# A chunked linear-attention kernel with a fused MLP: N of the chunk after next earlier in the order, its inverse stored by GpSimd, turned w ahead of the decay sums

## The chip, the cores and the metric

The kernel runs on one core of one Trainium2 chip. The metric is the device time of one execution in microseconds (us). A core has five engines that run side by side, each with its own instruction queue: TensorE (PE; its weight loads are shown apart as PEld), VectorE (DVE), ScalarE (ACT), GpSimd (POOL) and SyncE (SP), which here issues nearly all DMAs. Each queue is worked off in the order of the program.

## What is computed

Two blocks in a row. The first is a recurrence over 768 steps for 4 batches and 8 heads with a 40x40 state. The second is an MLP over 3072 tokens with an exact GELU.

```python
for t in range(S):                       # batch 4, n_heads 8, seq 768, head_dim 40
    kt, vt, rt = (k[:, :, t], v[:, :, t], r[:, :, t])
    wt, at, bt = (w[:, :, t], a[:, :, t], b[:, :, t])
    y[:, :, t] = np.einsum('bhd,bhde->bhe', rt, state)
    Sa = np.einsum('bhde,bhe->bhd', state, at)
    state_decay = state * wt[:, :, None, :] - np.einsum('bhd,bhe->bhde', Sa, bt)
    state = state_decay + np.einsum('bhd,bhe->bhde', vt, kt)
...
h = x @ w_in                             # x: y turned to (3072, 320); w_in: (320, 2048)
g = 0.5 * h * (1.0 + erf(h * inv_sqrt2))
return g @ w_out                         # w_out: (2048, 320)
```

## The kernel before

The sequence is cut into 12 chunks of 64 steps. Within a chunk the recurrence becomes products of small matrices; between chunks only the state goes on. The dependence of the steps of one chunk on each other is a strictly triangular matrix N per batch and head, and the kernel needs the inverse of the unit triangular matrix that belongs to it. 64 such matrices of 64x64 per chunk are inverted in two steps: the 32x32 blocks on the diagonal on GpSimd, and the corner between them on TensorE.

The order of every engine's queue is the order in which the program is written: the kernel turns the planner off for all five engines (`manual_schedule`) and interleaves by hand. The loop over `c` (line 1122) works on three chunks at once: chunk `c` itself, `n = c + 1` whose inverse is finished, and `n2 = c + 2` whose inputs are loaded and whose N is made. The MLP of a finished chunk is a generator (`mlp`, line 894) of eight pieces; each `fill()` issues the next piece. In the steady state the first four pieces are the first layer (`ph`, line 902, 40 matmuls each), the last four the second layer. For chunks from 3 on the second layer is done with seven half-size products in place of eight (`seven`, line 845): m1 and m2, then m5 and m6, then m3 and m7, then m4, at line 855. A pair of them takes about 4.5 us of TensorE. For chunks 0 to 2 it is the plain product (line 919), whose PSUM buffer is held over four pieces.

The steps that the change touches:

- `sums(c)`, line 407: from the logarithms of w, two sets of products on TensorE, the running sums (`cum`, four matmuls) and the same turned (`wT_ps`, 64 matmuls); then on ScalarE the exponentials `rw` (line 420), `wp` (422) and, for chunks from 4 on, `en` (427).
- `scale_b` (460, DVE), `scale_k` (467, GpSimd): b and k times `rw`. `scale_a` (477, DVE): turned a times `wp`. `turn_b` (489): turned b times `en`, two DVE instructions (176 and 495).
- `make_N(c)`, line 572: 64 matmuls, then DVE masks them into N (line 550), then SP issues four DMAs that write the diagonal blocks to DRAM (line 587).
- `start_inverse(c, nc.gpsimd)`, line 623: GpSimd clears W, SP reads the blocks back in another layout (Nb, line 636), and GpSimd does 31 columns of two operations each (lines 644 and 646).
- `store_inverse(c)`, line 652: two DMAs write W to DRAM (line 658), each of 64 partitions, with runs of 128 bytes on the DRAM side. `fetch_inverse(c)`, line 661: six DMAs read it back (lines 668 and 672) into Tt and T2.
- `turn_corner(c)`, line 679: one DVE transpose of Tt into L (line 681). `corner(c)`, line 683: 64 small matmuls J of N and L, the first work of TensorE in the next turn of the loop.
- `make_A`, `make_av`, `make_RV` for chunk n: 64 matmuls each; A and RV are masked by DVE (line 550), av is copied by ScalarE (line 618). A(n) and the turned b of n2 share one SBUF buffer.

PSUM is handed out as four buffers of two banks each (`duo`, line 90), and every product above takes one.

In the order before, SP meets, per turn: the loads of w, a, r, turned b, v and turned k of n2; eleven DMAs inside SBUF for x (lines 803 and 806); the store of the inverse of n; the loads of v, b and k of n2 (lines 200 and 153); the fetch of the inverse of n; one store of results; the stores of N of n2; the reads of Nb; another store of results.

Of the kernel before, what the change touches and what calls it, by code (L numbers as in the profile page):

```python
# [19 lines left out]
def kernel(  # L20
# [69 lines left out]
    def duo(name):  # L90
        return psum.tile([P, 2, 512], FP32, tag="duo", name=name)
# [7 lines left out]
    def mm(o, lhsT, rhs, first=True):  # L99
        nc.tensor.matmul(o, lhsT, rhs, start=first, stop=True, skip_group_check=True)  # L100
# [295 lines left out]
    def run(steps):  # L396
        for _ in steps:
            pass
# [7 lines left out]

    def sums(c):
        logw = raws.pop((c, "w"))
        cum = duo("cum")[:, :, :DM]
        for g in range(G):  # L410
            mm(cum[:, g], cum_m, logw[:, g * DM:(g + 1) * DM])

        pt = duo("wT_ps").rearrange("p e (n t) -> p e n t", t=C)
        for n in range(G * NP):
            for x in range(2):
                for e in range(2):
                    at = (2 * n + x) * D
                    mm(pt[half(x), e, n], logw[half(e), at:at + HP], cum_m[half(e), half(e)])
        rw = (avs_ring if c in (1, 2) else part_ring)()[:, :, :DM]
        nc.scalar.activation(rw, cum, ACT.Exp, scale=-1.0)  # L420
        wp = wp_ring()
        nc.scalar.activation(wp[:, :, 1:].rearrange("p (n e) t -> p e n t", e=2), pt, ACT.Exp)
        decays[c] = rw.rearrange("p g (h d) -> p g h d", h=H), wp
        turned_in.setdefault(c, {})["wp"] = wp
        if c >= NB:
            en = turned_in.setdefault(c, {})["en"] = by_batch(side("en", "kT", 1))
            nc.scalar.activation(en.rearrange("p (e n) t -> p e n t", e=2), pt, ACT.Exp, scale=-1.0)

    def flip(src, name):

# [414 lines left out]
    def seven(c, s1, s2):  # L845
        t1, t2, t4 = sums_of_w
        t3 = quarter(0, 1)
        os = [work.tile([P, 2, DM // 2], FP32, tag="os", name="os", bufs=2) for g in range(G)]
        c11, c12, c21, c22 = os[0][:, 0], os[0][:, 1], os[1][:, 0], os[1][:, 1]

        def products_of(*factors):
            po = duo("po")
            for n, (l_, r_) in enumerate(factors):
                for f in range(NF // 2):
                    nc.tensor.matmul(po[:, n, :DM // 2], l_[:, f], r_[:, f], start=f == 0, stop=f == NF // 2 - 1)  # L855
            return po[:, 0, :DM // 2], po[:, 1, :DM // 2]

        def add(to, one_, other):
            nc.vector.tensor_tensor(to, one_, other, ALU.add)  # L859

        def store(g):
            for e in range(2):
                row = (G * e + g) * S + c * C
                nc.sync.dma_start(out=out[row:row + C], in_=os[g][half(e)].rearrange("p z d -> p (z d)"))

        m1, m2 = products_of((block(0, 0), quarter(0, 0)), (block(0, 1), quarter(1, 0)))
        if s2 is None:
            s2 = SM_ring().rearrange("p e g n c -> p (e g n c)")[:, :NF * P // 2].rearrange("p (f t) -> p f t", t=P)
            nc.vector.tensor_tensor(s2, s1, block(0, 0), ALU.subtract)
        nc.vector.tensor_tensor(block(1, 0), block(0, 0), block(1, 0), ALU.subtract)  # L870
        nc.scalar.copy(c12, m1)
        nc.scalar.copy(c11, m2)
        add(c11, c11, c12)
        yield
        nc.vector.tensor_tensor(block(0, 1), block(0, 1), s2, ALU.subtract)  # L875
        m5, m6 = products_of((s1, t1), (s2, t2))
        nc.scalar.copy(c22, m5)  # L877
        add(c12, c12, m6)
        yield
        m3, m7 = products_of((block(0, 1), quarter(1, 1)), (block(1, 0), t3))  # L880
        add(c21, c12, m7)
        add(c12, c12, c22)
        add(c12, c12, m3)
        add(c22, c22, c21)
        store(0)
        yield
        m4, _ = products_of((block(1, 1), t4))
        add(c21, c21, m4)
        store(1)
        yield  # L890
# [3 lines left out]
    def mlp(c):  # L894
        xt = xts.pop(c)
        for q in range(NF // 4):
            ph = duo("ph").rearrange("p x (s t) -> p x s t", s=2)
            for s in range(2):
                p = 2 * q + s
                for kt in range(NK):  # L900
                    for x in range(2):
                        nc.tensor.matmul(ph[:, x, s], w_in_sb[half(x), kt, p * P:(p + 1) * P], xt[half(x), kt],  # L902
                                         start=kt == 0, stop=kt == NK - 1)
            nc.scalar.activation(gt[:, 4 * q:4 * q + 4].rearrange("p (x s) t -> p x s t", x=2), ph, ACT.Gelu)  # L904
            if c >= NS and q == NF // 4 - 1:
                s1, s2 = half_tile("conv", 2), None
                nc.vector.tensor_tensor(s1, block(1, 0), block(1, 1), ALU.add)  # L907
                if c >= NCH - 2:
                    s2 = half_tile("conv", 2)
                    nc.vector.tensor_tensor(s2, s1, block(0, 0), ALU.subtract)  # L910
            yield
        if c >= NS:
            yield from seven(c, s1, s2)
            return
        po = duo("po")[:, :, :DM]
        for part in range(2):
            for g in range(G):
                for f in range(NF // 2 * part, NF // 2 * (part + 1)):
                    nc.tensor.matmul(po[:, g], gt[:, f, g * P:(g + 1) * P], w_out_sb[:, f],  # L919
                                     start=f == 0, stop=f == NF - 1)  # L920
                if part:
                    os = work.tile([P, DM], FP32, tag="os", name="os", bufs=2)
                    nc.vector.tensor_copy(os, po[:, g])  # L923
                    for e in range(2):
                        row = (G * e + g) * S + c * C
                        nc.sync.dma_start(out=out[row:row + C], in_=os[half(e)])
                yield

# [193 lines left out]
    for c in range(2, NCH):  # L1122
        n, n2 = c + 1, c + 2
        more, more2 = n < NCH, n2 < NCH
        corner(c)
        make_X(c)
        if c == NS + 1:
            weight_sums(3)
        if c == 2:

            seconds(1, (14, 14), last=True)
            fill()
            turn_b(n)
            make_N(n)
            run(start_inverse(n, nc.gpsimd))
            load_r(n)
            load_v(n)
        else:
            fill()
        if more2:  # L1140
            load_next(n2)
        joined(c)
        if c == 2:
            pieces.reverse()
            seconds(2, last=True)
        fill()
        make_sa(c)
        make_saT(c)
        if c == 2:
            turn_r(n)  # L1150
            scale_k(n, nc.vector)
            fill()
            pieces.reverse()
            fill(2)
            turn_k(n)
        if more2:
            load_r(n2)
        if more2:
            turn_a(n2)
            fetch_pairs(n2, "b_turned", b, nc.sync, False, paired["a"])  # L1160
        fill()
        make_y2(c)
        make_M(c)
        if more:
            turn_v(n)
        if more2:
            load_v(n2)
            turn_r(n2)
            fetch_pairs(n2, "k_turned", k, nc.sync, False, paired["r"])
        fill()  # L1170
        if more2:
            logs(n2)
        make_QY(c)
        outputs(c)
        pieces.append(mlp(c))
        fill()
        if c == NS:
            weight_sums(0)
            weight_sums(1)
        if more:  # L1180
            make_A(n)
            store_inverse(n)
        if more2:
            load_VR(n2)
            load_kb(n2)
            sums(n2)
        if more:
            turn_state()
        if more2:
            scale_a(n2)  # L1190
        fill()
        if more:
            fetch_inverse(n)
            make_av(n)
        if c == NS:
            weight_sums(2)
        if more2:
            turn_b(n2)
        if more:
            make_RV(n)  # L1200
        if more2:
            scale(n2)
        fill()
        if more:
            turn_corner(n)
        if more2:
            make_N(n2)
            run(start_inverse(n2, nc.gpsimd))
        if more2:
            turn_k(n2)  # L1210
        fill()
# [31 lines left out]
```

## Time and profile before

| | us |
|---|---|
| median of 3 runs | 751.65 |
| lowest, highest | 749.77, 757.06 |
| the profiled execution, its own time | 747.88 |
| its span, first to last instruction | 746.2 |
| PE busy | 677.1 (91%) |
| PEld, DVE busy | 588.7, 385.7 |
| POOL, ACT busy | 333.0, 214.3 |
| mean granted TensorE clock | 0.933 |

The profile is of one execution. A line of a timeline gives start, duration, engine, line of the kernel, operation, the tile written and the tiles read, and how many instructions were merged; in brackets the idle time of the engine before it and what ended it. "SPq" is the queue in which SP issues DMAs: its durations are those of the issue, not of the transfer. "PEclk" is the TensorE clock that was granted, 1.00 or 9 and more tenths being full.

### The profile page before, as it was taken

To read this page: it belongs to the slowest core of one execution; us is meant where nothing else is said; L and a number is where in the kernel's file an instruction comes from. 1 tells how busy PE (TensorE), PEld (TensorE's weight loads), DVE (VectorE), ACT (ScalarE), POOL (GpSimd) and SP (SyncE) were. 2 spreads that over 40 slices of the span, in tenths; PEclk is the share of its full clock that TensorE was granted. 3 is DMA by queue.
4 is the path that set the end of the run, shared out by engine and by line. 5 is a ranking of instruction groups with operands and counts; after the bars stand their busy time and mean duration, and the time that the engine had idled before them with its cause. 6 is when DMAs were issued, how large, how long until landed. Compare 5 with 4: busy or idle time off the path is not lost.

```text
span 746.2 us, 31351 instructions
## 1 busy us (share of the span) xinstructions
PE 677.1 (91%) x14096; PEld 588.7 (79%) x14096; DVE 385.7 (52%) x541; ACT 214.3 (29%) x279; POOL 333.0 (45%) x776
## 2 busy tenths in 40 slices
PE   7356889669999999999997999989999979999997
PEld 5355678557777877898896898887998978998987
DVE  2777389873335365474544464643563653531403
ACT  5124463523141241332231332232232312112020
POOL 3385168700831852842842833834833833810000
PEclk9655799679999999999998999998999998999999
DMA  9797659453756657556646565656556553030000
GB/s 120 131 178 139 122 120 237 80 116 81 130 108 125 110 106 131 99 107 129 117 79 116 106 106 116 120 86 132 100 99 129 102 88 64 16 57 4 20 18 19
DMA packets 302159, 75.76 MB, mean 102 GB/s; under 512 B 290408, under 2 KB 295304, under 8 KB 302024
## 3 DMA queue, kind: packets, MB, share of 16 engines
q1 hardware_dynamic: 301824, 73.58, 52.5%
q8 instruction: 111, 1.82, 1.0%
q14 instruction: 24, 0.20, 0.1%
q10 hardware_dynamic: 200, 0.16, 0.1%
HBM read 59.54 MB, written 10.22 MB: 93 GB/s over the span
## 4 chain that ended last, share of the span: by engine, by line
PE 49%; POOL 14%; SPq 13%; DMA 7%; DVE 7%; issue 6%; ACT 2%; ACTq 1%; DVEq 0%; POOLq 0%
PE ph L902 20%; PE po L919 7%; PE po L855 6%; POOL W L646 6%; POOL tmp L644 5%; SPq L153 4%; PE QY L100 3%; DMA Nb<-N 2%; DMA Tt<-inv 2%; SPq L668 2%; PE X L100 2%; PE J L100 2%; DMA N<-N 2%; SPq L806 1%; SPq L200 1%
## 5 line engine op out<-in xcount | busy, mean ns | idle before, releaser
L902 PE MATMUL ph<-xt,w_in_sb 64*128 64x256 f32 x1920 | 227.1, 389 | 0.7 <-ACT gt L904 0.4
L902 PEld LDWEIGHTS ph<-xt,w_in_sb 64*128 64x128 f32 x1920 | 186.9, 191 | 26.3 <-issue 1.8
L644 POOL TENSOR_TENSOR tmp<-W,Nb 128x126 f32<-128x126 f32 (+22 forms) x310 | 127.3, 411 | 137.6 <-DMA Nb<-N 114.0
L646 POOL TENSOR_TENSOR W<-W,tmp 128x126 f32<-128x126 f32 (+22 forms) x310 | 131.5, 424 | 24.3
L904 ACT ACTIVATE gt<-ph 128x1024 f32<-128x1024 f32 x48 | 49.1, 1023 | 149.2 <-PE ph L902 124.3
L855 PE MATMUL po<-w_out_sb,gt 128*128 128x160 f32 x576 | 82.9, 302 | 0.1
L855 PEld LDWEIGHTS po<-w_out_sb,gt 128*128 128x128 f32 x576 | 78.7, 190 | 2.2 <-DVE gt L875 0.4
L919 PE MATMUL po<-w_out_sb,gt 128*128 128x320 f32 x192 | 57.4, 454 | 0.6 <-DVE os L923 0.6
L471 POOL TENSOR_TENSOR k_rows<-k_rows,part 128x640 f32<-128x640 f32 x8 | 12.4, 1549 | 98.4 <-DMA Tt<-inv 86.8
L919 PEld LDWEIGHTS po<-w_out_sb,gt 128*128 128x128 f32 x192 | 37.0, 198 | 16.6 <-issue 2.3
L550 DVE TENSOR_TENSOR SM<-M_ps,upper 128x1024 f32<-128x1024 f32 x12 | 14.7, 1223 | 49.6 <-PE M_ps L100 49.6
L711 DVE COPY Tt<-J 32x512 f32<-32x512 f32 x12 | 8.3, 689 | 60.4 <-ACT Tt L711 60.3
L695 ACT COPY Js<-J 128x256 f32<-128x256 f32 x12 | 4.5, 371 | 100.5 <-PE J L100 100.5
L907 DVE TENSOR_TENSOR half<-gt 128x1024 f32<-128x1024 f32 x9 | 11.6, 1285 | 38.6 <-ACT gt L904 38.6
L100 PE MATMUL J<-L,N 32*32 32x32 f32 x768 | 10.2, 205 | 22.4 <-DVE L L681 22.4
L100 PEld LDWEIGHTS J<-L,N 32*32 32x32 f32 x768 | 8.9, 116 | 25.0 <-issue 25.0
L904 ACT ACT_TABLE_LOAD x10 | 12.8, 1283 | 47.7 <-PE ph L902 47.7
L303 ACT ACTIVATE conv<-conv,rebias 128x320 uint32<-128x320 uint32 (+1 forms) x26 | 16.0, 624 | 35.5 <-DVE conv L302 35.3
L859 DVE TENSOR_TENSOR os<-os,po 128x160 f32<-128x160 f32 x36 | 11.5, 319 | 28.2 <-ACT os L877 14.2
L855 PE MATMUL po<-extra,half 128*128 128x160 f32 x176 | 25.4, 299 | 0.0
L739 DVE COPY SM<-sap 128x640 f32<-128x640 f32 x12 | 9.9, 824 | 28.2 <-PE sap L100 28.1
L855 PEld LDWEIGHTS po<-extra,half 128*128 128x128 f32 x176 | 24.2, 190 | 0.0
(196 smaller groups left out, 1129.2 us busy)
## 6 DMA issues: line engine op xcount, KB each, us to landing
Nb<-N SPq DMA_DIRECT2D x22, 256.0 KB
VR<-in_v_dram SPq DMA_DIRECT2D x24, 160.0 KB
out_dram<-os SPq DMA_DIRECT2D x48, 80.0 KB
w_tile<-in_w_dram SPq DMA_DIRECT2D x22, 160.0 KB
b_rows<-in_b_dram SPq DMA_DIRECT2D x22, 160.0 KB
k_rows<-in_k_dram SPq DMA_DIRECT2D x22, 160.0 KB
w_out_sb<-in_moe_w_out_dram SPq DMA_DIRECT2D x11, 320.0 KB
N<-N SPq DMA_DIRECT2D x48, 64.0 KB
```

The lines of the kernel that those rows point to most:

```text
L100: nc.tensor.matmul(o, lhsT, rhs, start=first, stop=True, skip_group_check=True)
L153: eng.dma_start(out=t[half(e)].rearrange("p g h d -> p (g h) d")[:, :, :D], in_=rows_of(src, c, e))
L303: nc.scalar.activation(power, power, ACT.Relu, bias=rebias, scale=8.0)
L471: eng.tensor_tensor(to, raws.pop((c, "k")), rwv, ALU.mult)
L550: nc.vector.tensor_tensor(to, pt, upper.unsqueeze(1).to_broadcast([P, 2 * G * NP, C]), ALU.mult)
L644: eng.tensor_tensor(t, W[:, :rows, j:j + 1].to_broadcast([P, rows, rest]), Nb[:, j:j + 1, j + 1:].to_broadcast([P, rows, rest]), ALU.mult)
L646: eng.tensor_tensor(W[:, :rows, j + 1:], W[:, :rows, j + 1:], t, ALU.add)
L668: engs[j % len(engs)].dma_start(out=flat(Tt)[at:at + BL, :, z * BL:(z + 1) * BL], in_=inv[j, z].rearrange("n s t -> s n t"))
L855: nc.tensor.matmul(po[:, n, :DM // 2], l_[:, f], r_[:, f], start=f == 0, stop=f == NF // 2 - 1)
L902: nc.tensor.matmul(ph[:, x, s], w_in_sb[half(x), kt, p * P:(p + 1) * P], xt[half(x), kt], start=kt == 0, stop=kt == NK - 1)
L904: nc.scalar.activation(gt[:, 4 * q:4 * q + 4].rearrange("p (x s) t -> p x s t", x=2), ph, ACT.Gelu)
L919: nc.tensor.matmul(po[:, g], gt[:, f, g * P:(g + 1) * P], w_out_sb[:, f], start=f == 0, stop=f == NF - 1)
```

## The change

In `sums`, the turned products and their exponentials come first, and the sums and `rw` last. In the loop, `make_av(n)` with the fetch moves ahead of the second pair of half products, `turn_b(n2)` too, and `make_N(n2)` with the start of its inverse moves ahead of the third pair; `scale(n2)` now follows N. The store of the inverse is issued by GpSimd directly behind the inverse, where SP issued it a turn later. In `seven`, m5 and m6 are issued before one subtraction; in the plain second layer both halves are copied out and stored after the last product.

```diff
     def sums(c):
         logw = raws.pop((c, "w"))
-        cum = duo("cum")[:, :, :DM]
-        for g in range(G):
-            mm(cum[:, g], cum_m, logw[:, g * DM:(g + 1) * DM])
-
         pt = duo("wT_ps").rearrange("p e (n t) -> p e n t", t=C)
...
-        rw = (avs_ring if c in (1, 2) else part_ring)()[:, :, :DM]
-        nc.scalar.activation(rw, cum, ACT.Exp, scale=-1.0)
+        cum = duo("cum")[:, :, :DM]
+        for g in range(G):
+            mm(cum[:, g], cum_m, logw[:, g * DM:(g + 1) * DM])
         wp = wp_ring()
         nc.scalar.activation(wp[:, :, 1:].rearrange("p (n e) t -> p e n t", e=2), pt, ACT.Exp)
-        decays[c] = rw.rearrange("p g (h d) -> p g h d", h=H), wp
         turned_in.setdefault(c, {})["wp"] = wp
         if c >= NB:
             en = turned_in.setdefault(c, {})["en"] = by_batch(side("en", "kT", 1))
             nc.scalar.activation(en.rearrange("p (e n) t -> p e n t", e=2), pt, ACT.Exp, scale=-1.0)
+        rw = (avs_ring if c in (1, 2) else part_ring)()[:, :, :DM]
+        nc.scalar.activation(rw, cum, ACT.Exp, scale=-1.0)
+        decays[c] = rw.rearrange("p g (h d) -> p g h d", h=H), wp
...
+        m5, m6 = products_of((s1, t1), (s2, t2))
         nc.vector.tensor_tensor(block(0, 1), block(0, 1), s2, ALU.subtract)
-        m5, m6 = products_of((s1, t1), (s2, t2))
         nc.scalar.copy(c22, m5)
...
-                if part:
+                for last in range(G if part and g else 0):
                     os = work.tile([P, DM], FP32, tag="os", name="os", bufs=2)
-                    nc.vector.tensor_copy(os, po[:, g])
+                    nc.vector.tensor_copy(os, po[:, last])
                     for e in range(2):
-                        row = (G * e + g) * S + c * C
+                        row = (G * e + last) * S + c * C
                         nc.sync.dma_start(out=out[row:row + C], in_=os[half(e)])
...
             run(start_inverse(n, nc.gpsimd))
+            store_inverse(n, (nc.gpsimd,))
             load_r(n)
...
         if more:
             make_A(n)
-            store_inverse(n)
         if more2:
             load_VR(n2)
             load_kb(n2)
             sums(n2)
         if more:
             turn_state()
+            fetch_inverse(n)
+            make_av(n)
         if more2:
             scale_a(n2)
+            turn_b(n2)
         fill()
-        if more:
-            fetch_inverse(n)
-            make_av(n)
         if c == NS:
             weight_sums(2)
-        if more2:
-            turn_b(n2)
         if more:
             make_RV(n)
         if more2:
+            make_N(n2)
             scale(n2)
-        fill()
+            run(start_inverse(n2, nc.gpsimd))
+            store_inverse(n2, (nc.gpsimd,))
         if more:
             turn_corner(n)
-        if more2:
-            make_N(n2)
-            run(start_inverse(n2, nc.gpsimd))
+        fill()
         if more2:
             turn_k(n2)
         fill()
```

## The prediction

> **What bounds the kernel now.** I read the page first. Its busy line and its 40 slices show TensorE nearly full after the first fifth of the span:
>
> ```profile
> PE 677.1 (91%) x14096; PEld 588.7 (79%) x14096; DVE 385.7 (52%) x541; ACT 214.3 (29%) x279; POOL 333.0 (45%) x776
> PE   7356889669999999999997999989999979999997
> ```
>
> The reader is to see three slices below 9 late in the PE row: TensorE sets the pace and stops now and then. So I asked for the waits of PE from 280 us to the end (columns: total us, times, longest). There is one line only:
>
> ```profile
> PE J L100 <- DVE L L681: 11.9, 3, 4.1
> ```
>
> J (`corner`) waits for L, the turned corner of the inverse (`turn_corner`). Next I cut the span at the starts of J, one stretch per chunk (columns: us, busy time by engine, then PEclk):
>
> ```profile
> 289.20:340.20 51.00, 51.00 (x1181) 46.15 (x1180) 27.17 (x33) 15.51 (x20) 27.29 (x64) 1.00 0.62 114
> 340.20:395.70 55.50, 51.52 (x1181) 46.30 (x1181) 29.28 (x35) 15.50 (x20) 29.76 (x69) 1.00 0.59 109
> 395.70:450.40 54.70, 54.61 (x1180) 48.40 (x1180) 29.41 (x35) 15.50 (x20) 27.67 (x66) 0.94 0.58 107
> 450.40:505.30 54.90, 51.14 (x1181) 46.19 (x1181) 28.55 (x35) 15.51 (x20) 28.17 (x63) 1.00 0.57 109
> 615.40:665.70 50.30, 50.27 (x1048) 45.70 (x1048) 21.41 (x28) 9.77 (x14) 27.23 (x66) 0.94 0.22 43
> ```
>
> The first row is a chunk without loss: 51.0 us. The second waits 4 us at its end at full clock; the third does not wait, but its clock is 0.94 and it costs the same 3.7 us. They alternate. The timeline of PE shows why:
>
> ```profile
> 395.70 0.74 PE L100 MATMUL J<-L,N 32*32 32x32 f32 x64 [3.98 <-DVE L L681]
> 396.37 1.82 PE L100 MATMUL X<-st,aT 40*64 40x40 f32 x64
> 398.12 7.61 PE L902 MATMUL ph<-xt,w_in_sb 64*128 64x256 f32 x40
> 406.35 4.59 PE L902 MATMUL ph<-xt,w_in_sb 64*128 64x256 f32 x40
> ```
>
> Straight after the wait the same 40 matmuls take 7.61 us instead of 4.59, and X takes 1.82 instead of 1.14. This slow stretch gives the inverse the time that it lacks, so the next J finds L ready; the clock is then full, and the one after waits again.
>
> **Why L is late.** The loop of the inverse, from the timelines of POOL, SP and DVE (start, duration):
>
> ```profile
> 350.62 0.24 POOL L644 TENSOR_TENSOR tmp<-W,Nb 128x31 f32<-128x31 f32 x1 [9.86 <-DMA Nb<-N]
> 382.22 0.23 POOL L646 TENSOR_TENSOR W<-W,tmp 128x16 f32<-128x16 f32 x1
> 382.47 1.30 SPq L658 DMA_DIRECT2D inv<-W  x2
> 383.87 2.60 SPq L200 DMA_DIRECT2D VR<-in_v_dram  x2
> 389.88 2.45 SPq L668 DMA_DIRECT2D Tt<-inv  x4
> 394.86 0.70 DVE L681 STREAM_TRANSPOSE L<-Tt 128x512 f32<-128x512 f32 x1
> ```
>
> GpSimd ends the inverse at 382.45, 31.8 us after it began. SP stands at the store until then and issues it; behind it in SP's order are the loads of v, b and k, so the fetch of the inverse starts at 389.88, 7.4 us after the end. From there to the end of L are 5.7 us. The other half: N is masked at 340.57, its stores begin at 340.60, and GpSimd starts on it at 350.62, 10.0 us later. N's stores stand in SP's order behind the fetch and behind one output store (338.61 to 339.8).
>
> **The change, part by part.** Times count from a J, with 51.0 us to the next; the base is the chunk from 289.2.
>
> 1. *N ahead of m3 and m7.* N's products ended at 337.9; ahead of them now goes no third pair (4.5 us), so they end near 333.2. What N needs is ready: scale_a and turn_b move up too, 1.23 + 1.25 + 1.22 us of DVE behind the exponentials, done near 329.0. On DVE the mask no longer follows turn_corner, scale_b and four L859 additions, so N is masked near 334.3 instead of 340.57. SP now sets the start: it reaches the fetch 1.4 us earlier (the store left its queue), at 333.0, issues its six DMAs until 337.1, then N's four stores, 3.5 us earlier than before. GpSimd starts at 347.1, which is 6.9 after the next J instead of 10.4.
>
> 2. *The store on GpSimd.* Two DMAs, each of 64 partitions in 1024 runs of 128 bytes. Queued behind them on GpSimd are scale_k and the cleared W of the next chunk; these wait for k and then the new N for over 10 us anyhow (POOL idle 10.78 us before k_rows), so gain nothing and lose nothing below that. SP gets 1.3 us and no longer stands at the store with v, b and k behind it (five waits on W, 15.2 us in all). No POOL DMA is in this trace. Nearest row: the store of an earlier chunk, issued by an SP that stood ready; W ended at 146.20 and its landing released POOL's memset at 150.15, so **4.0 us** from end to landing. The page "DMA: Bandwidth & Descriptors" of the Trainium skill (Latency and other measured facts) gives about 1 us to the first byte for a GpSimd DMA and 0.6 on the SP path; by it an estimate of 4.4. But the page "SBUF — State Buffer" (A bandwidth-pool intuition that's wrong) speaks against this edit: GpSimd cannot write descriptors while DVE runs a two-port operation, 3.1 us in place of 0.62. For two DMAs that is 5 us more, 9.4. The DVE rows near the end of the inverse are masks, additions and tensor_tensor, with no copy, so I lean to the lower. Below 4.0 I see no reason (the same bytes land by the same 16 engines). What 2048 runs cost in software neither row nor page prices; I let the upper end be 15 us, SP's 1.3 us taken tenfold. I take **5**.
>
> 3. *The loop that follows.* GpSimd 31.8, store 5, fetch issue 4.1, N to GpSimd 10.0: 50.9 us against 51.0. In place of the 7.4 us between W and fetch stand 5. From 6.9: end at 38.7, landed at 43.7; SP comes to the fetch at 43.8; L 5.7 later at 49.5, less 0.9 of additions that no longer precede it (by the chain Tt landed at 393.93, L began at 394.86). J at 51.0 need not wait. **Gain**: the five stretches 340.2 to 615.4 come to 275.2 us, at 51.0 each 255.0: 20.2. The last row carries the slow clock alone, 3.2. Sum **23.4 us**; the earlier stall before the loop (5.8 us at 159.6) is untouched.
>
> 4. *av ahead of m5 and m6.* The 4.5 us pair covered A's mask. Now turned w (1.1), sums (1.3) and the state's turn (1.0) cover it: A's products end at 321.7, av could start at 325.1, the mask ended at 324.15. Covered, with 0.9 to spare; without that cover up to 1 us per chunk.
>
> 5. *Turned w first.* Inside the loop wp and en come about a microsecond earlier, rw later; scale_b has long waited for b instead. m5's PSUM buffer may wait for en: 0.15 us times seven. In chunks 2 and 3 one buffer of four is held by the long product, and av waits about 1.1 us twice (my estimate from exponentials of 1.28 + 1.03 + 1.03). In the first chunk rw moves from 9.12 to about 10.1; scale_b, then nT by TensorE, lose 0.3 us. Sum **2.7 us**, between 0 and 8.
>
> 6. m5 and m6 issued before the subtraction, and both copies of the long product after its second half: the same instructions on each queue; nothing waits between them. Zero; if the copies were late, 0.5 us in two chunks.
>
> Together: 23.4 - 2.7 = 20.7 us. The profiled execution took 747.88 us (span 746.2); it becomes about 727.2. The median of the three runs is 751.65, 3.8 above it; taken along, **731 us**.
>
> **Rivals.**
> *A, GpSimd's store is too dear (slower).* The loop is 45.9 + s, s from W's end to landing. From s = 5.1 a chunk waits, and each microsecond of s costs one per chunk. The chunks now average 55.0, so at s = 9.1 the change only breaks even. At s = 13 a chunk takes 58.9, six of them +23 us: 775. For: 2048 short runs by software, no row; DVE is 52% busy. Against: the gaps between GpSimd's operations are 0.07 us, and nothing queued behind needs it at once.
> *B, in part.* s of 6 to 8: chunks of 52 to 54 us, waits of 1 to 3 us. At 53 that is 2 x 6 = 12 us, plus the clock of the last chunk: about 739. A wait of 1.03 us in chunk 2 (before tn) left matmuls at normal length, so short waits should not cost clock.
> *C, SP stays the bound (same).* SP's rows in this chunk sum to about 44 of 51 us, and from the v loads (22.6 after J) to the end of the fetch there is no gap. If the earlier N meets longer issues (r loads vary from 3.94 to 6.55 us), small waits return, and with them the clock: 748 to 752.
>
> **How the numbers follow.** Full gain, 726 to 735: 0.42. B, 735 to 744: 0.20. C and the middle of A: 0.12. A, slower by over 7.5 us: 0.26. From 726 to 764 takes in all but 0.05 below and about 0.15 of A above; the likeliest alone is 726 to 735. One per cent (7.5 us) is about what a measurement of this kernel can tell, its runs being 749.77 to 757.06. Faster 0.62, same 0.12, slower 0.26.
>
> **What would show it.** Right: no J <- L line for PE after 280 us, stretches of 51 us at clock 1.00, N masked some 6 us before J, GpSimd starting 6 to 7 us after it, and landing within 5 us of W's end. Wrong: fetches on SP waiting for inv by POOL's queue for over 4 us (A), av or m5 as new waits of PE (parts 4 and 5), or L late with the landing long done (C).

## The result, and the profile after

| | before | after |
|---|---|---|
| median of 4 runs each | 752.15 | **727.96** |
| lowest, highest | 749.77, 757.06 | 725.91, 732.97 |
| profiled execution, its span | 747.88, 746.2 | 726.3, 724.5 |
| PE, POOL busy | 677.1, 333.0 | 663.1, 352.8 |
| mean granted TensorE clock | 0.933 | 0.946 |

The ratio is 0.968, with a 95% interval of 0.9608 to 0.9753: faster by 2.5 to 3.9%. 731 was forecast, with 726 to 735 as the likeliest stretch. Some executions are slower for reasons outside the kernel: the ratios here and below leave them out, the medians do not, and the profile of e12 below, taken in one of them, is not compared.

First the page of the changed kernel: its busy line, its PE slices, its clock, and the two DMA queues of data.

```profile
PE 663.1 (92%) x14096; PEld 582.5 (80%) x14096; DVE 383.5 (53%) x541; ACT 213.8 (30%) x279; POOL 352.8 (49%) x794
PE   6455889569999999999999999999999999999997
PEclk9655799779999999999999999999999999999999
q1 hardware_dynamic: 283104, 71.22, 52.0%
q0 software_dynamic: 864, 2.36, 1.8%
```

The three weak slices of PE are gone, and behind the prologue no digit of the clock is below 9. GpSimd's stores are the new queue q0. PE has the same 14096 matmuls and is busy 14 us less: that part of the gain is mostly clock. The rest is mostly waits. The waits of PE from 230 us on (total us, times, longest):

```profile
PE J L100 <- DVE L L680: 3.4, 4, 1.0
PE av L100 <- DVE A L549: 1.0, 1, 1.0
```

J still waits for L, but four times for at most 1.0 us where it waited three times for up to 4.1. The stretches from J to J (us, busy time by engine, PEclk, DMA share, GB/s), with two rows and then one left out by "...":

```profile
285.70:336.40 50.70, 50.70 (x1181) 46.18 (x1180) 28.41 (x35) 15.42 (x20) 30.02 (x68) 1.00 0.65 117
...
437.90:489.50 51.60, 50.77 (x1181) 46.17 (x1181) 28.61 (x34) 15.40 (x20) 31.73 (x68) 1.00 0.61 115
...
541.40:594.80 53.40, 52.49 (x1185) 47.45 (x1189) 28.42 (x35) 15.41 (x20) 32.07 (x68) 0.97 0.60 112
594.80:644.20 49.40, 47.80 (x1049) 43.51 (x1050) 20.74 (x28) 9.77 (x14) 27.78 (x64) 1.00 0.22 44
```

The clock is 1.00 in all but one, and a chunk without loss takes 50.7 us. Toward the end small losses return. From the timelines of PE, POOL and SP I took this table; all but the first two columns count from the chunk's J, and W is the inverse on GpSimd:

| J at | to the next | W starts | W ends | fetch starts | N masked | N's stores start |
|---|---|---|---|---|---|---|
| 285.7 | 50.7 | 3.3 | 34.2 | 43.0 | 45.6 | 47.4 |
| 336.4 | 50.7 | 5.3 | 35.5 | 43.3 | 45.6 | 48.1 |
| 387.1 | 50.7 | 7.5 | 38.5 | 45.5 | 45.6 | 49.8 |
| 437.9 | 51.6 | 9.1 | 41.8 | 48.3 | 45.6 | 51.4 |
| 489.5 | 51.9 | 10.5 | 43.2 | 48.5 | 45.7 | 51.5 |
| 541.4 | 53.4 | 10.1 | 43.1 | 49.8 | 47.2 | 53.0 |

The loop of the inverse, from one start of W to the next, takes 51.5 to 53.0 us in these rows (336.4 + 5.3 - 285.7 - 3.3 = 52.7), against 50.7 for a chunk. So W starts some 2 us later in each chunk, until at 9 to 10 after J its L is late. In the first three rows this does not come round through W, which ended 7 to 9 us before the fetch: SP has only then finished the loads of v, b and k, and N's stores stand behind the fetch. From SP's timeline in the first row:

```profile
326.95 1.68 SPq L153 DMA_DIRECT2D k_rows<-in_k_dram  x2
328.74 2.40 SPq L667 DMA_DIRECT2D Tt<-inv  x4
```

From the fourth row on the landing of the store decides; SP then stands at the fetch. From the waits of SP from 230 to 650 us:

```profile
SPq L667 <- DMA inv<-W: 23.7, 4, 9.3
```

The store itself, from the timeline of POOL, the line of its group (count, then ns min, median, max), and what is told of its landing:

```profile
533.02 1.63 POOL L657 DMA_DIRECT2D inv<-W  x2 [0.30 <-POOL W L645]
...
L657 POOL DMA_DIRECT2D inv<-W x18: 822/823/962, 211.7 to 636.4; - x18
...
DMA to landing us min/median/max: 3.4/4.4/5.5
```

Each of the two DMAs holds GpSimd for 0.82 us, and lands a median 4.4 us after its issue.

### The profile page after: what moved, and what is told of

Read it like the earlier page. It is cut to its first block, busy times and chain, and to the rows that moved or that the text cites. A ratio compares the mean times of both kernels' runs of the same rounds, so it can differ in the third digit from the quotient of the medians.

```text
span 724.5 us, 31335 instructions
## 1 busy us (share of the span) xinstructions
PE 663.1 (92%) x14096; PEld 582.5 (80%) x14096; DVE 383.5 (53%) x541; ACT 213.8 (30%) x279; POOL 352.8 (49%) x794
## 4 chain that ended last, share of the span: by engine, by line
PE 49%; POOL 19%; DMA 10%; SPq 7%; DVE 7%; issue 5%; ACT 2%; ACTq 1%; DVEq 0%; POOLq 0%
PE ph L901 17%; POOL W L645 8%; POOL tmp L643 8%; PE po L918 8%; PE po L854 7%; PE QY L100 3%; DMA inv<-W 3%; DMA N<-N 3%; DMA Nb<-N 2%; PE cum L100 1%; PE J L100 1%; POOL st L643 1%; SPq L153 1%; POOL st L645 1%; PE X L100 1%
## 5 line engine op out<-in xcount | busy, mean ns | idle before, releaser
L901 PE MATMUL ph<-xt,w_in_sb 64*128 64x256 f32 x1920 | 221.1, 383 | 0.8 <-ACT gt L903 0.8
L901 PEld LDWEIGHTS ph<-xt,w_in_sb 64*128 64x128 f32 x1920 | 183.4, 188 | 23.9 <-ACT gt L903 0.5
L643 POOL TENSOR_TENSOR tmp<-W,Nb 128x126 f32<-128x126 f32 (+22 forms) x310 | 129.7, 418 | 128.4 <-DMA Nb<-N 104.9
L645 POOL TENSOR_TENSOR W<-W,tmp 128x126 f32<-128x126 f32 (+22 forms) x310 | 133.7, 431 | 24.3
L918 PE MATMUL po<-w_out_sb,gt 128*128 128x320 f32 x192 | 55.3, 444 | 0.0
L549 DVE TENSOR_TENSOR VR<-RV_ps,upper 128x1024 f32<-128x1024 f32 x12 | 14.7, 1224 | 17.3 <-PE RV_ps L100 17.3
L680 DVE STREAM_TRANSPOSE L<-Tt 128x512 f32<-128x512 f32 x12 | 8.5, 711 | 27.4 <-DMA Tt<-inv 27.4
```

The source lines that it names most:

```text
L549: nc.vector.tensor_tensor(to, pt, upper.unsqueeze(1).to_broadcast([P, 2 * G * NP, C]), ALU.mult)
L643: eng.tensor_tensor(t, W[:, :rows, j:j + 1].to_broadcast([P, rows, rest]), Nb[:, j:j + 1, j + 1:].to_broadcast([P, rows, rest]), ALU.mult)
L645: eng.tensor_tensor(W[:, :rows, j + 1:], W[:, :rows, j + 1:], t, ALU.add)
```

## The experiments

Each profile starts with a prologue that varied by several us between executions with no relation to the edit (first instruction to the J of chunk 2: 157.1 to 166.2 us). So beside the medians I compare "the loop": that J to the end of the profiled span.

| | median us (runs) | ratio to before, 95% | loop, us | J waits after 230 us (times, longest) |
|---|---|---|---|---|
| before | 752.15 (4) | 1 | 586.6 | 11.9 (3, 4.1) |
| after | 727.96 (4) | 0.968 [0.9608, 0.9753] | 565.1 | 3.4 (4, 1.0) |
| e1_sp_store | 743.41 (10) | 0.9915 [0.9871, 0.9959] | 580.6 | 11.9 (4, 4.2) |
| e2_pool_store | 739.12 (4) | 0.9846 [0.9795, 0.9897] | 579.6 | 5.8 (5, 2.0) |
| e4_late_2 | 734.22 (4) | 0.9743 [0.9661, 0.9826] | 567.5 | 3.2 (3, 1.6) |
| e10_late_5 | 749.19 (10) | 0.9978 [0.9941, 1.0016] | 581.0 | 10.3 (6, 3.9) |
| e5_after_short | 725.91 (4) | 0.9688 [0.9611, 0.9765] | 560.4 | none |
| e6_before_short | 731.85 (4) | 0.9778 [0.9676, 0.988] | 567.2 | 0.4 (2, 0.2) |
| e7_sums_only | 753.31 (10) | 1.0061 [1.0017, 1.0106] | 596.2 | 14.2 (5, 4.2) |
| e9_old_sums | 727.17 (4) | 0.9688 [0.9631, 0.9745] | 567.6 | 1.4 (2, 1.0) |
| e3_n_by_act | 775.77 (4) | 1.0329 [1.0275, 1.0383] | 611.4 | 30.1 (8, 13.2) |
| e8_n_by_pool | 721.87 (4) | 0.9647 [0.9579, 0.9714] | 563.2 | 1.1 (1, 1.1) |
| e11_after_again | 729.75 (6) | 0.9752 [0.9717, 0.9787] | 565.8 | 4.3 (4, 1.7) |
| e12_n_by_pool_again | 726.11 (6) | 0.9686 [0.9638, 0.9734] | not compared | |

The **theory**: TensorE is held up by the loop of the inverse, which runs through SP's queue; the store on GpSimd and the earlier N each shorten it, and the slow clock follows from its waits. The **rivals**: one of the two does it all; or the clock has a cause of its own. Of the expectations below, e8, e10 and e11 came out in their range; e1, e4, e6, e7 and e12 missed it by up to 1.4 us, and e2, e3, e5 and e9 by more.

### Each half alone

e1: the changed kernel, with SP issuing the store again.

```diff
-            store_inverse(n, (nc.gpsimd,))
...
             make_A(n)
+            store_inverse(n)
...
-            store_inverse(n2, (nc.gpsimd,))
```

> The changed kernel with the store of the inverse issued by SP again, behind A of chunk n as before; N stays early, turned w stays first. Theory (the loop of the inverse is what TensorE waits for, and SP's queue is half of it): SP stands at the store until GpSimd ends and then has v, b and k between store and fetch, about 7.4 us from W's end to the fetch instead of the 5 to 6.7 of the changed kernel, so the loop is 31.8 + 7.4 + 4.1 + 10 = 53.3 us: waits of 2 to 3 us before J return in chunks 5 to 10, 735 to 742 us. Rival (N's earlier place alone brings the gain): 726 to 730, no more J waits than in the changed kernel.

e2: the kernel before, with only the store moved to GpSimd.

```diff
             run(start_inverse(n, nc.gpsimd))
+            store_inverse(n, (nc.gpsimd,))
...
             make_A(n)
-            store_inverse(n)
...
             run(start_inverse(n2, nc.gpsimd))
+            store_inverse(n2, (nc.gpsimd,))
```

> The kernel before with one edit: GpSimd issues the store directly behind the inverse; N, av, turned w stay where they were. Theory: the fetch starts 6 us after W's end in place of 7.4, but N still follows the fetch, one output store and L, so the loop is 31.8 + 6 + 6.9 (fetch start to N's stores) + 10 = 54.7 against chunks of 55.0 before: 745 to 751 us, J waits of about 4 us remaining. Rival (the store's place in SP's queue is the whole cause): most of the gain, 728 to 735.

With everything but the store 0.85% is gained, with the store alone 1.5%, with both 3.2%; the first two are each under 2%, but their intervals leave out no change. Neither half does it all. N was not moved without turned b, av and the sums, so e1 does not tell these apart. Four stretches of e1 show the pattern of the kernel before again:

```profile
334.90:389.70 54.80, 50.81 (x1183) 46.21 (x1183) 28.12 (x33) 15.42 (x20) 30.12 (x67) 0.99 0.62 110
389.70:443.60 53.90, 53.49 (x1185) 48.36 (x1189) 28.33 (x35) 15.42 (x20) 28.07 (x66) 0.94 0.59 110
443.60:497.70 54.10, 50.79 (x1184) 46.20 (x1185) 28.44 (x35) 15.42 (x20) 30.07 (x67) 1.00 0.60 111
497.70:551.60 53.90, 53.90 (x1181) 48.62 (x1181) 28.67 (x36) 15.43 (x20) 28.86 (x68) 0.94 0.60 111
```

A chunk that waits (busy 50.8 of 54 to 55 us) takes turns with one of slow clock (busy all through, 0.94). In e1 the fetch again starts 7.6 to 9.2 us after W's end in these chunks and the next, and J waits 11.9 us. In e2 N's stores begin only 52.5 to 56 us after J, so GpSimd still starts late. I had expected e2 at 745 to 751; its gain was larger. In its five chunks from 338.5 us on the fetch starts 5.9 to 8.8 us after W's end (7.4 to 9.3 before), J waits 2.0 us at most, and the clock stays at 0.97 to 1.00; a gain in clock was not in my sum for e2.

### How dear may the store be?

GpSimd clears a dead buffer two times (e4, 1.96 us) or five times (e10, 5.0 us) ahead of the store.

```diff
     def store_inverse(c, engs=...):
+        if engs[0] is nc.gpsimd:
+            for _ in range(2):           # e10: range(5)
+                nc.gpsimd.memset(old_N[c], 0.0)
```

> The changed kernel with two idle clearings of Nb (about 1 us each) on GpSimd between the inverse and its store, so that the store leaves some 2 us later; nothing else moves. Theory (past its slack the loop costs one for one): chunks 5 to 10 grow from 50.7 to 53.4 to about 53 to 55.5, plus clock after waits of about 1 us or more, 735 to 745 us. Rival (the loop has slack, TensorE sets the time): 726 to 731.

> The changed kernel with five clearings of Nb, 0.98 us each by the run with two, ahead of the store on GpSimd: 4.9 us in all. Theory (the loop costs one for one past its slack; two clearings took 1.9 us and were mostly taken up by an earlier landing): loop 51.9 + 4.9 = 56 or so, chunks 5 to 10 of 54 to 56, with clock loss: 746 to 760. Rival (landing waits for quiet of the DMA engines, not for GpSimd, so a later store lands at the same time): 730 to 738.

Two clearings cost the loop only 2.4 us (567.5 against 565.1) in six chunks, where one for one would be near 12. Part of it was made up: in three late chunks W took 31.1 to 32.6 us for 32.6 to 33.0, and the landing came a median 4.1 us after the issue for 4.4. So one for one is not shown here; the median of 734.22 lies just below what I expected. Five cost it 15.9 us and bring the kernel back to the time of before. From the timeline of POOL in e10, then the waits of its PE:

```profile
482.76 5.00 POOL L657 MEMSET Nb<- 128x1024 f32 x5
487.71 1.63 POOL L662 DMA_DIRECT2D inv<-W  x2
```

```profile
PE J L100 <- DVE L L685: 10.3, 6, 3.9
```

Nothing but GpSimd's lateness differs from the changed kernel, and J waits three times as much. From 334.9 us on the fetch starts 9.2 to 11.5 us after W's end, 10.2 on average, and the kernel is as fast as before. So the break-even that I had put at a landing of 9.1 us lies near 10. (The profiled execution of e10, at 739.89, is the fastest of its ten runs, so the loop in its row is rather too short.)

### A shorter inverse

The other term of the loop: 23 of the 31 columns from chunk 3 on, in the changed kernel (e5) and in the one before (e6).

```diff
-            for j in range(BL - 1):
+            for j in range(BL - 1 if c < 3 else 23):
```

> The changed kernel with the inverses of chunks 3 to 11 cut to their first 23 of 31 columns (8 columns are left out, some 8 us of GpSimd per chunk). Theory: the loop falls to about 44 us, below TensorE's 50.7; no J wait after chunk 3, clock 1.00, all chunks 50.7, some 7 us below the changed kernel: 718 to 723. Rival (what is left is not the loop): 726 to 730.

> The kernel before with the same 8 columns left out in chunks 3 to 11. Theory (the waits and the slow clock behind them are all from the loop of the inverse): chunks of 51.0 at clock 1.00, the 23.4 us of my sum vanish: 726 to 731. Rival (the alternating clock has a cause of its own, load or temperature): the waits vanish, about 12 us, but stretches at clock 0.94 remain: 736 to 742.

Five stretches of e6, that is of the order before with a shorter inverse:

```profile
340.90:392.00 51.10, 51.06 (x1181) 46.11 (x1180) 28.91 (x35) 15.51 (x20) 22.86 (x50) 1.00 0.65 118
392.00:444.60 52.60, 51.55 (x1184) 46.35 (x1187) 28.42 (x35) 15.51 (x20) 20.46 (x48) 1.00 0.60 112
444.60:495.80 51.20, 51.10 (x1184) 46.17 (x1184) 28.05 (x35) 15.50 (x20) 22.34 (x50) 1.00 0.62 116
495.80:547.50 51.70, 51.41 (x1180) 46.36 (x1181) 29.27 (x35) 15.50 (x20) 23.91 (x54) 1.00 0.64 117
547.50:599.40 51.90, 51.71 (x1180) 46.44 (x1180) 28.31 (x35) 15.50 (x20) 21.08 (x48) 1.00 0.60 112
```

The reader is to compare the clock with that of e1: 1.00 throughout, though nothing was done to TensorE's work. With the loop shortened, the waits and the slow clock of the kernel before both go; the rival of a clock with its own cause falls. The loop of e6 is 19.4 us shorter than before, somewhat under the 23.4 that I gave all its losses. In e5 no J waits at all, and its loop is 4.7 us shorter than in the changed kernel (5.4 shorter than in e11): that is what this still loses to the inverse. The median of e5, 725.91 where I had expected 718 to 723, hardly shows it; in the profile its prologue took 4 us longer.

e5 also shows where the late starts of W come from. Its W is some 8 to 11 us shorter and no fetch waits for the landing, yet from the J at 290.3 us on W starts 4.4, 5.8, 7.7, 9.0 and 9.8 us after J, much as in the changed kernel. From POOL's timeline in the fourth of these chunks (J at 442.49):

```profile
451.44 0.24 POOL L643 TENSOR_TENSOR tmp<-W,Nb 128x31 f32<-128x31 f32 x1 [8.31 <-DMA Nb<-N]
473.98 1.63 POOL L657 DMA_DIRECT2D inv<-W  x2 [0.30 <-POOL W L645]
```

So it is the way of N to GpSimd behind SP's queue, and not the length of W, that makes W start later; the length of W decides whether J then has to wait. (In the sixth chunk of e5 W starts at 6.4 again. Why this way takes longer in some chunks is open.)

### The order of the decay sums

e7: the kernel before with the new `sums` alone. e9: the changed kernel with the old `sums`.

```diff
-        cum = duo("cum")[:, :, :DM]
...
         pt = duo("wT_ps").rearrange("p e (n t) -> p e n t", t=C)
...
+        cum = duo("cum")[:, :, :DM]
```

> The kernel before with only the turned w ahead of the decay sums, in every chunk. Theory: off the loop, 749 to 753, with 0.3 us lost in the first chunk and scale_a about a microsecond earlier. Rival (the exponentials delay N in the loop): 745 or less.

> The changed kernel with the decay sums ahead of the turned w again; all else as changed. Theory (with av ahead of m5 and m6 TensorE reaches m5 before the exponential en has freed m5's PSUM buffer, if cum and rw come first): en ends about 1.3 + 0.7 us later, so m5 waits up to 2 us in each chunk, 735 to 744, with waits of PE behind ACT en. Rival (the order in sums does not matter, as alone in the kernel before): 726 to 731.

e9 took 727.17 us, so the order in `sums` is not needed for the gain, and my expectation of a loss fell. Its undisturbed chunks take 51.0 us, those of the changed kernel 50.7: 0.3 us a chunk, too little for the medians. In e7 alone it was 0.6% slower than before, and its profile has one stretch of 60.6 us. The new wait there, from the waits of PE, and what stood on DVE, from its timeline:

```profile
PE po L918 <- DVE os L922: 4.8, 1, 4.8
```

```profile
286.39 0.82 DVE L463 SCALAR_TENSOR_TENSOR b_rows<-b_rows,part 128x640 f32<-128x640 f32 x1 [6.29 <-DMA b_rows<-in_b_dram]
287.14 0.48 DVE L922 COPY os<-po 128x320 f32<-128x320 f32 x1
```

SP stood at the store of W until 275.87, so b landed late; scale_b held DVE for 6.29 us, and the copy that frees PE's PSUM buffer stood behind it. That is one execution; whether it happens in all of e7's runs is open.

### N's stores out of SP's queue

If SP's queue is what is left of the loop, N's four stores behind the fetch are next. e3 gives them to ScalarE, e8 to GpSimd; e12 is e8 again, beside the changed kernel (e11) on one chip.

```diff
-    def make_N(c):
+    def make_N(c, eng=nc.sync):
...
-                nc.sync.dma_start(out=blk[j, z]...
+                eng.dma_start(out=blk[j, z]...
...
-            make_N(n2)
+            make_N(n2, nc.scalar)        # e8, e12: nc.gpsimd
```

> The changed kernel with N's four stores issued by ACT in the loop. In the changed kernel N is masked 45.6 us after J, but its stores stand in SP's order behind the fetch, which waits for the landing of GpSimd's store; GpSimd's start drifts from 3.3 to 10.5 us after J, until J waits again by 0.7 to 1.0 us. Theory (that queue closes the loop): without it GpSimd starts at 3 to 5 in every chunk, no wait of J after chunk 3, chunks of 50.7, and 5 to 7 us less: 720 to 724. Rival (TensorE alone sets the time now, the remaining waits are noise): 726 to 730. Rival (ACT's queue is blocked by the stores): waits behind ACT, over 730.

> The changed kernel with N's four stores issued by GpSimd in the loop. With ACT as issuer GpSimd did start at 3.6 to 4.1 us after J, but the load of k on SP waited for the landing of N, since DMAs of SP and ACT take turns on the same eight completion counters; GpSimd's own DMAs have other counters. Theory (the queue behind the fetch closes the loop): GpSimd stores N at 45.6 to 49 after J whatever the fetch does, starts at about 6.5 in every chunk without drift, no J wait after chunk 3 and chunks of 50.7: 720 to 726. Rival (the four software stores land so late that nothing is won): GpSimd starts at 9 or later, 727 or more.

> The changed kernel itself, beside the next one on the same chip: 724 to 733, and how far its stretch before the J of chunk 2 and its drift of GpSimd's start differ from one execution to another.

> N's four stores on GpSimd, again, beside the changed kernel on the same chip. Theory: the 4 to 6 us that the drift costs in chunks 7 to 11 are won, so 4 to 7 us below the changed kernel. Rival (the difference seen was one between chips and builds): within 2 us of it.

e3 is 3.3% slower, the largest miss of the study. GpSimd starts 4 us after J, as I had expected, but that is of no use: the fetch starts only 49 to 55 us after J. From the waits of SP, then its timeline in one chunk, then ScalarE's:

```profile
SPq L153 <- DMA N<-N: 36.2, 7, 6.5
```

```profile
460.38 1.85 SPq L153 DMA_DIRECT2D b_rows<-in_b_dram  x2
468.71 1.35 SPq L153 DMA_DIRECT2D k_rows<-in_k_dram  x2
470.17 2.44 SPq L667 DMA_DIRECT2D Tt<-inv  x4
```

```profile
465.71 3.29 ACTq L586 DMA_DIRECT2D N<-N  x4
```

SP stands for 6.5 us before the load of k, which has nothing to do with N, until the stores of the next N begin to land. The trace names the completion counter of each DMA: those of SP and of ScalarE take turns on the same eight, and those of GpSimd have eight others. In this chunk the first load of k has the counter of the first of ScalarE's stores; that was issued at 465.71, and the load leaves at 468.71, 3.0 us later. So SP here waits for ScalarE. That the shared counter is the cause is read from this; ScalarE with counters of its own was not tried.

e8, where GpSimd has its own counters, bears this out: W starts 2.4 to 6.5 us after J with no drift, J waits once, and the stretches are at the floor:

```profile
392.30:443.00 50.70, 50.70 (x1181) 46.16 (x1180) 27.28 (x33) 15.41 (x20) 31.16 (x71) 1.00 0.62 118
443.00:493.70 50.70, 50.70 (x1181) 46.17 (x1180) 29.08 (x37) 15.40 (x20) 33.57 (x75) 1.00 0.63 118
493.70:544.60 50.90, 50.90 (x1181) 46.27 (x1180) 28.10 (x34) 15.41 (x20) 31.87 (x71) 1.00 0.63 118
```

Its loop is 1.9 us shorter than that of the changed kernel, and 2.6 shorter than in e11, by one profile of e8. In the medians e8 came out 6.1 us lower on another chip, e12 3.6 us lower than e11 on the same one (726.11 against 729.75); the intervals of these two overlap ([0.9638, 0.9734] and [0.9717, 0.9787]). Of the kernels that invert N in full it is the fastest by both medians, but half a per cent is at the edge of what was measured here.

## Why the prediction was right, step by step

**What bounds the kernel** held: e6 shows that the inverse's loop makes the waits and the slow clock, e10 that the loop's length, past its slack, decides the time.

**1, N ahead.** N was to be masked some 45.1 us after J; it is at 45.6. GpSimd was to start 6.9 after J; it starts at 3.3 to 10.5, for the drift of part 3. By e1 and e2 this step, with all that moved along with it, is worth 0.85% alone and 1.7% on top of the store, of 3.2%.

**2, the store.** This was the widest unknown. From W's end to the fetch, where the landing decides, are 5.3 to 6.7 us; I took 5 between bounds of 4.0 and 15. What was short is the landing. The row of 4.0 us holds the issue of both DMAs by SP, and the second landed 3.3 us after its issue (146.84 to 150.15). GpSimd issues its second 0.30 + 0.82 us after W's end, and with the median landing of 4.4 this makes 5.5. The estimate of 4.4 us that I drew from the page "DMA: Bandwidth & Descriptors" of the Trainium skill (Latency and other measured facts) also counts from W's end, so it was about 1.1 us short. My other estimate, 9.4, from "SBUF — State Buffer" (A bandwidth-pool intuition that's wrong), where a GpSimd DMA takes 3.1 us beside a DVE copy and 0.62 alone, was not put to the test: of the DVE rows that overlap the 18 issues none is a copy, and no issue took over 0.96 us. Rival A's break-even of 9.1 is borne out, or nearly: with the clearings of e10 the landing comes some 10 us after W's end, and the gain is gone.

**3, the loop.** Its gain was forecast at 23.4 us and is **17.8**; this is the term of the sum that was mis-sized. The five stretches that ran from 340.2 were to take 255.0 us and take 258.3 (50.7 + 50.7 + 51.6 + 51.9 + 53.4); the last was to take 47.1 and takes 49.5. I had balanced the loop at 50.9 against 51.0, and it is 51.5 to 53.0, while the floor fell to 50.7. In the last three chunks before 594.8, where it closes through the landing, the terms are 32.6 to 33.0 us for W (mine 31.8), 5.3 to 6.7 for the landing (5), 3.0 to 3.2 from the fetch to N's stores (4.1) and 10.0 to 10.7 from there to GpSimd (10.0). In the three chunks before these the landing has slack, and it is N's way behind SP's queue that makes W start later. Then small waits return: rival B in miniature, as it foresaw chunks of 52 to 54. One sentence of B is wrong, though, "short waits should not cost clock". From the timeline of PE:

```profile
541.37 0.74 PE L100 MATMUL J<-L,N 32*32 32x32 f32 x64 [0.98 <-DVE L L680]
542.04 1.14 PE L100 MATMUL X<-st,aT 40*64 40x40 f32 x64
543.12 6.28 PE L901 MATMUL ph<-xt,w_in_sb 64*128 64x256 f32 x40
```

After a wait of 0.98 us the 40 matmuls took 6.28 us for 4.59. Within them the granted clock, the third figure from the end, fell to 0.50:

```profile
545.00:547.00 2.00, 2.00 (x12) 1.60 (x12) 0.77 (x2) 0.00 (x0) 0.00 (x0) 0.50 0.01 2
```

After the other three waits, of 0.65 to 0.91 us, they took 4.59. So the one wait cost 0.98 + 1.69. Nor does the length tell: in e2 a wait of 1.15 us was followed by 6.20 us, one of 1.99 by 4.59.

**4, av.** Covered in every chunk with `sums`, as forecast. In the last chunk there are none, and the cover is gone: av waits 0.96 us there, the "up to 1 us" of the prediction, which I had not put into the sum for that chunk.

**5, turned w first.** I charged 2.7 us; the chunks without loss became 0.3 us shorter instead (50.7 for 51.0), and e9 with the old order has 51.0 again. No wait for `en` appears.

**6, m5, m6 and the copies.** Neither was run alone; the loop of the later chunks shows nothing of them. But the stretch of chunk 2 to 3, which I left untouched, fell from 76.6 to 73.4 us. Its waits on `part` (1.03 us) and on `os` (0.58) are gone; e9, with the old `sums`, still has the first, and e7, with the new ones alone, lacks the first but has the second (0.82). So the first goes with part 5, the second with the rest of the change, by place with the copies. About 1.4 us more are the slow matmuls behind the wait of 5.8 us with which this stretch begins, 5.89 us for 7.25; these are chance and not the change, for in e11, the same kernel, they take 7.08.

The sum of the span: -17.8 for the loop, -3.2 for chunk 2, -0.5 for the next two, -0.2 around: -21.7, against -20.7. Two errors, 5.6 us too much in the loop and some 6 us too little elsewhere (2.7 charged, 3.2 + 0.5 not seen), nearly cancelled, and 1.4 us of the second are the chance of part 6. So it is in part luck that 731 came so near to 727.96: the forecast is better than its steps.

**Rival C**, SP stays the bound, is half true: SP's loads set the fetch at 43.0 to 45.5 after J in three chunks, and N's stores behind it set the start of W there, which e5 shows apart from W's length. Its time of 748 to 752 did not come. e8, with N's stores out of SP's queue, has W start at 2.4 to 6.5 without drift.

## What to carry to other kernels

When an engine waits for a loop that runs through several queues, sum the loop, term by term, against the time between its uses: here 51.5 to 53.0 us against 50.7 go with a drift, three clean chunks and then small waits. Then ask in each chunk which term really came last; a loop can slip by one queue alone, as here by SP's, before it closes. A change that shortens only one part gained less than half. An in-order queue that stands at one store delays the loads behind it; give the store to the engine that makes its data, where that engine has nothing urgent next. Moving a DMA to another queue can also tie two queues together, so look at what the old queue waits for afterwards, not only at when the moved DMA goes out.

## What the runs showed of the hardware

- A GpSimd DMA of 1024 runs of 128 bytes was issued in 0.82 us (after), against 0.63 us for the same from SP (before), and landed a median 4.4 us (3.4 to 5.5) after its issue; GpSimd's stores of N took 0.66 us and landed in 2.8 (e8).
- DMAs from ScalarE held up SP for up to 6.5 us at a load with no data in common (e3).
- Waits of TensorE of about 1 us could lower its clock: after 0.98 us (after) and 1.15 us (e2) the granted clock fell to 0.50 for some 2 us or more, and 40 matmuls took 6.28 and 6.20 us for 4.59. After 1.03 us (before), 1.19 (e11) and 1.99 (e2) nothing of the kind followed.
